# In the fourth step, VectorE takes the outputs of the third unit ahead of the last two pieces of words, and ScalarE scales the last piece behind the evictions of k and q

## The chip, the core and the metric

The kernel runs on one core of a Trainium2 chip. A core has five engines that run side by side and meet at semaphores: TensorE (PE in the profile, with PEld for its weight loads), VectorE (DVE), ScalarE (ACT), GpSimd (POOL) and SyncE (SP, which here only issues DMAs). Each engine works off its own queue in the order in which the program wrote it. The metric is the device time of one execution in microseconds (us); the time of a kernel is the median over its runs.

## The reference

Two blocks follow each other. The first is an mLSTM cell over 4 batches, 8 heads, 768 tokens and a head width of 40, written as a recurrence:

```python
m_new  = np.maximum(f[t] + m, i[t])
f_stab = np.exp(f[t] + m - m_new);  i_stab = np.exp(i[t] - m_new)
C = f_stab * C + i_stab * outer(v[t], k[t])
n = f_stab * n + i_stab * k[t]
y[t] = sigmoid(o[t]) * (C @ q[t]) / max(|n . q[t]|, 1)
```

Its output, seen as x with 3072 tokens of width 320, goes through a feed-forward block of width 1024, all in float32:

```python
h   = ((x @ w1) * (x @ w2)) @ w3
out = h @ w_out
```

The four weight matrices come as 64-bit floats. The kernel reads each number as two 32-bit words and makes a 32-bit float of them itself.

## The kernel before, in words

**Units and steps.** The 3072 tokens are cut into 24 units: unit n is a run of 128 tokens of one batch, all 8 heads. The main loop runs over 32 steps, s = 0 to 31. In step s TensorE, within `quarter_work`, computes the outputs of unit s-1 (products of its masked weights with v, and of q with the states: the tiles `ph` and `pi`, printed as `cell`), then the scores of unit s (`ss`) and its contributions to the state (`pc`). Behind them come the turning of y (`x_trans`, tile `px`) and of k and q of the next unit (`turn`, tile `pt`). Ahead of them come the matmuls of the feed-forward block that are due in the step: `up` multiplies x with 256 columns of w1 and of w2 over the first 256 of the 320 rows (tiles `pa` and `pb`), and `up_rest` adds the last 64 rows, for which the weights lie in a tile of their own, `wr` (line 623), and multiplies both results.

**The fourth and the fifth step.** "The fourth step" is s = 3; the third unit is n = 2, whose outputs are taken there. The feed-forward matmuls of s = 2 and 3 use columns 0 to 511 of the weights, those of s = 4 start on columns 512 to 1023 (f = 4, 5 of `ups`).

**The words.** A weight matrix is fetched in pieces of 512 columns (`fetch`). The ten pieces of w1, w2 and `wr` are listed in `w12`: columns 0 to 511 of w1 (two row blocks), of w2 (two) and of `wr`, and then the same for columns 512 to 1023. A piece is fetched as words into a `raw` tile by a DMA that SP issues, scaled by two instructions of ScalarE (`scale`, lines 188 and 192; `scale_next` takes the next fetched piece), and put together by two instructions of VectorE (`to_f32`, lines 196 and 197; `convert` takes the next scaled piece, and scales one itself if none is waiting). The last two pieces are the second row block of w2 (a tile printed as `w`) and `wr`, both for columns 512 to 1023. The `raw` tiles are four, used in turn; a fetch waits until VectorE is done with the piece that lay there.

**Who sets the order.** From `front` on, every engine but TensorE is held to the order in which the program wrote its instructions (`keep_order`, line 539), and TensorE has its own chain of order (`in_order`). So the place of a `convert()` in the text is its place in VectorE's queue. In step 3 both pieces are converted in `rest()` (lines 876 to 878), ahead of `outputs(2)`. VectorE's outputs are the instructions at lines 414, 421, 429, 431, 432, 434 and 436; between them stand the masking of the scores (line 390, needed by TensorE for the outputs of the next step), the state (lines 399 and 405, with GpSimd's decay at line 332 between them) and, at the end of the step, `rows_of_u` (line 292).

**Counters.** `n_cvt` says how many pieces are converted at the end of each step, and `converted` how many have been, which decides how far `fetch` runs ahead.

Of the kernel before, what the change touches and what calls it, by code (L numbers as in the profile page):

```python
# [16 lines left out]
def kernel(  # L17
# [166 lines left out]
    def scale(raw, early):  # L184


        lo, hi = raw[:, :, 0], raw[:, :, 1].bitcast(FP)
        nc.scalar.activation(out=hi, in_=hi, func=AF.Prelu, scale=2.0 ** -111, alpha=2.0 ** 32)
        if early:
            nc.vector.tensor_scalar(out=lo, in0=lo, scalar1=2.0 ** -29, scalar2=2.0 ** 23, op0=OP.mult, op1=OP.add)  # L190
        else:
            nc.scalar.activation(out=lo, in_=lo, func=AF.Copy, scale=2.0 ** -29, bias=2.0 ** 23)

    def to_f32(dst, raw):
        bits, V = dst.bitcast(U32), nc.vector
        V.tensor_scalar(out=bits, in0=raw[:, :, 1], scalar1=3, scalar2=None, op0=OP.logical_shift_left)
        V.tensor_tensor(out=bits, in0=bits, in1=raw[:, :, 0], op=OP.add)  # L197
# [32 lines left out]
    def scale_next(early=False):  # L230
        scaled.append(pend.pop(0))
        scale(scaled[-1][1], early)

    def convert():
        if not scaled:
            scale_next()
        dst, raw, ko, half = scaled.pop(0)
        if dst is not None:
            to_f32(dst, raw)
            return  # L240
        w3 = wst.tile([128, CW], FP, name="w3", tag="w3")
        to_f32(w3, raw)
        if half == 0:
            w3T_t[ko] = wst.tile([128, FO, 128], FP, name="w3T", tag="w3T")
        nc.vector.transpose(out=w3T_t[ko].rearrange("c k (m r) -> c m k r", r=32)[:, 2 * half:2 * half + 2],
                            in_=w3.rearrange("r (m c k) -> r m k c", m=2, k=FO))
        if half:
            turned_w3.append(ko)
# [59 lines left out]
    def turn(n):  # L308


        if n >= N_DVE:
            for src, dst, name in zip(turned_in[n % 2], (kT_t, qT_t), ("kT", "qT")):
                dst[n] = sb.tile([128, NP, P], FP, name=name, tag=name)
                done = nc.vector.transpose(out=dst[n].rearrange("i p (r f) -> i p f r", f=4),
                                           in_=src[:, 32:TB].rearrange("i (p f d) -> i p f d", p=NP, f=4)[:, :, :, 0:32])
            return done
        for src, dst, name in ((kbuf[n % NB], kT_t, "kT"), (qbuf[n % NBQ], qT_t, "qT")):
            pt = mps([128, NP, P], "pt")
            for p in range(NP):
                transpose(pt[:, p, :], src[:, 2 * p:2 * p + 2, :].rearrange("p a b -> p (a b)"))  # L320
            dst[n] = sb.tile([128, NP, P], FP, name=name, tag=name)
            nc.scalar.copy(out=dst[n], in_=pt)
# [9 lines left out]
        nc.gpsimd.tensor_tensor(out=new, in0=old, op=OP.mult, in1=decay[:, b * NP:(b + 1) * NP, 2 * c + x:2 * c + x + 1]  # L332
                                .to_broadcast([P, NP, D1]))

    def quarter_work(s, rest, between):


        rest()

        def part(j, c0, n):  # L340
            return cell[j][:, :, c0:c0 + NP * n].rearrange("p x (n d) -> p x n d", d=n)

        ss, pc, pi = part(0, 0, L), part(0, NP * L, D1), part(1, 0, D1)
        ph = [cell[1][:, x, NP * D1:2 * NP * D1].rearrange("p (h d) -> p h d", d=D1) for x in range(2)]
        n = s - 1
        if 0 <= n < NU:
            pw, vt, qT = u_t.pop(n), vbuf[n % NBV], qT_t.pop(n)
            before = before_t.pop(n)

            if n < N_DIAG:  # L350
                ph = mps([P, H, D1], "ph")
                for hq in range(H):
                    for r in halves:
                        mm(ph[r, hq, :], pw[r, hq, :], vt[r, hq, :])
            for hd in range(H // 2 if n >= N_DIAG else 0):
                for x, e in quarters:
                    hq = hd if x == e else hd + H // 2
                    mm(ph[x][halves[e], hd, :], pw[halves[x], hq, :], vt[halves[x], hq, :])
            for p in range(NP):
                for hip, x in quarters:  # L360
                    mm(pi[halves[x], hip, p, :], qT[heads[hip], p, halves[x]], before[x][heads[hip], p, :])
        den = None
        if 0 <= s - 1 < NU:
            den = outputs(s - 1, pi, ph)
            den()
            if between:
                for _ in range(3):
                    den()
                den = None
                between()  # L370
        n, first_read = s, None
        if n < NU:
            c, b = divmod(n, B)
            kt, vw = kbuf[n % NB], vw_t.pop(n)
            ends = range(2 if c < NT2 - 1 else 1)
            first, second, after = state[b]
            before_t[n] = first, second
            state[b] = after, second, first
            kT, qT, pw = kT_t.pop(n), qT_t[n], u_t[n]
            for p in range(NP):  # L380
                for hip, x in quarters:
                    mm(ss[halves[x], hip, p, :], kT[heads[hip], p, halves[x]], qT[heads[hip], p, halves[x]])
            M = D if n else L
            for p in range(NP):
                for x, e in quarters:
                    if x in ends:
                        mm(pc[e * L:e * L + M, x, p, :], kt[halves[x], 2 * p + e, 0:M], vw[halves[x], 2 * p + e, :])
        if n < NU:
            pv = pw.rearrange("p (n two) t -> p two n t", two=2)
            first_read = nc.vector.tensor_tensor(out=pv, in0=ss, in1=pv, op=OP.mult)  # L390
        with tc.issue_after(first_read.ins) if first_read else nullcontext():
            if den:
                den()
            if n < NU:

                if c:
                    nc.vector.tensor_tensor(out=second, in0=pc[:, 0], in1=second, op=OP.add)  # L397
                else:
                    nc.vector.tensor_copy(out=second, in_=pc[:, 0])
                if len(ends) > 1:  # L400
                    decayed(after, second, n, 1)
            if den:
                den()
            if n < NU and len(ends) > 1:
                nc.vector.tensor_tensor(out=after, in0=pc[:, 1], in1=after, op=OP.add)
            if den:
                done = den()
        return done if den else first_read
# [390 lines left out]
    n_out = [0] * 27 + [1, 0, 1, 0, 3]  # L799
    w12 = [("w12", i, part) for part in range(2) for i in range(2 * KF + 1)]  # L800
    todo = w12[5:] + [("wo", i, 0) for i in range(FO)] + [("w3", ko, part) for ko in range(FO) for part in range(2)]
    n_cvt = [0, 0, 2, 0, 1, 2, 3, 3, 3] + [2] * 6
    n_fetch = [5, 5, 10]
    pinned, ahead = 32, 9
    behind = ExitStack()
    turned, converted, fetched = 0, 2, 5

    for s in range(len(n_up)):
# [62 lines left out]
        def rest():  # L871
            for x in open_ups:
                up_rest(*x)
            if seven:
                seven[2]()
            if s == 3:
                for _ in range(2):
                    convert()

        def between():  # L880
            twice(1)
            weighted(2)
            rows_of_u(3)
            for _ in range(3):
                scale_next()
            for n in range(2):
                x_trans(n)
                if n == 0:
                    warm(5)
            for _ in range(3):  # L890
                convert()
            turn(2)
            block = up(*now[0])
            weighted(3)
            weights(3)
            masks(3)
            out_gate(2)
            convert()
            up_rest(*block)

        gated = None
        if s <= NU:
            gated = quarter_work(s, rest, between if s == 2 else None)
        else:
            rest()
        with tc.issue_after(gated.ins) if gated else nullcontext():
# [11 lines left out]
            if N_DVE <= s + 1 < NU:  # L918
                gated = turn(s + 1)
# [10 lines left out]
            cell_psum.close()  # L930
            banks.extend([ps_m] * 3 + [ctx.enter_context(tc.tile_pool(name="ps_x", bufs=4, space=bass.MemoryType.PSUM))] * 4)
        if s in (2, 3):
            turned, converted = 2, converted + (4 if s == 2 else 2)
        if s + 1 < N_DVE:
            while turned < min(s - 1, NY):
                x_trans(turned)
                turned += 1
            if s not in (1, 2):
                turn(s + 1)
        if s < NU:  # L940
            if 0 < s < NU - 1 and s != 2:
                if s != 1:
                    weighted(s + 1)
                weights(s + 1)
                if 2 < s < N_DVE:
                    twice(s - 1)
                masks(s + 1)
            if s != 2:
                out_gate(s)
# [50 lines left out]
```

## Time and profile before

| | |
|---|---|
| median of 3 runs | 429.05 us (428.34, 429.05, 430.54) |
| profiled execution, its own time | 428.51 us |
| its span on the engines | 426.5 us |
| mean granted TensorE clock | 0.988 |
| TensorE busy | 411.7 us (97%) |
| VectorE busy | 313.0 us (73%) |
| ScalarE busy | 149.7 us (35%) |
| GpSimd busy | 154.6 us (36%) |

The profile is of one execution. Its span runs from the first to the last instruction of the engines; 2.0 us of the execution's own time lie outside it. In a timeline each line has a start in us from the span's start, a duration in us, the engine, the line of the kernel, the operation and the tiles (written from read), how many instructions were merged into it, and in brackets how long the engine had stood idle before it and what ended that. A list of waits gives for each pair of waiter and releaser the total in us, the number of times and the longest. In a table by stretches each line has the busy time and number of instructions of each engine, then the granted TensorE clock as a share of full speed, then the busy share of the DMA engines and what they moved.

### The profile page before, as it was taken

How to read it: one execution, taken by the hardware profiler on the slowest of the kernel's cores; microseconds unless marked ns; L12 is line 12 of the kernel's file. 1: busy time of each engine (PE TensorE's matmuls, PEld its weight loads, DVE VectorE, ACT ScalarE, POOL GpSimd, SP SyncE). 2: the span in 40 equal slices, each digit the busy share in tenths (PEclk: the TensorE clock that was granted, in tenths of full speed). 3: DMA queues.
4: the chain of work that ended last, by engine and by line, in shares of the span. 5: the costliest groups of instructions: out<-in, count | busy, mean ns of one | idle time of the engine just before them, and what ended most of it. 6: DMA issues, size and time to landing. Idle time of an engine off the chain costs nothing.

```text
span 426.5 us, 13080 instructions
## 1 busy us (share of the span) xinstructions
PE 411.7 (97%) x5353; PEld 337.9 (79%) x5353; DVE 313.0 (73%) x634; ACT 149.7 (35%) x404; POOL 154.6 (36%) x211
## 2 busy tenths in 40 slices
PE   7799789999999999999999999999999999999996
PEld 5788678887688788787777778788778779888896
DVE  6676787888949769778736966596878699575971
ACT  4866665567724523630333313132311110210000
POOL 4530232233303203303307743646363587542100
PEclk9879999999999999999999999999999999999999
DMA  8989878597997775886435585656421120000001
GB/s 189 227 169 233 210 126 147 132 197 180 210 205 135 166 181 132 179 162 111 83 85 129 136 147 129 142 135 113 96 39 36 35 38 2 31 2 31 2 32 61
DMA packets 135211, 51.15 MB, mean 120 GB/s; under 512 B 109360, under 2 KB 126960, under 8 KB 135152
## 3 DMA queue, kind: packets, MB, share of 16 engines
q1 hardware_dynamic: 131552, 46.29, 52.7%
q10 hardware_dynamic: 3600, 4.03, 2.7%
q8 instruction: 42, 0.69, 0.7%
q14 instruction: 17, 0.14, 0.1%
HBM read 44.50 MB, written 5.80 MB: 118 GB/s over the span
## 4 chain that ended last, share of the span: by engine, by line
PE 77%; DVE 7%; issue 5%; DMA 5%; SPq 4%; ACT 1%; POOL 0%; DVEq 0%; POOLq 0%; ACTq 0%
PE cell L92 20%; PE pa L92 18%; PE pb L92 12%; PE wp L92 8%; PE o L92 8%; PE po L92 4%; PE p L92 3%; DVE w3T L654 1%; DMA wo<-in_moe_w_dram 1%; PE px L95 1%; SPq L150 1%; DMA yb<-y_d 1%; DMA y_d<-y 1%; PE pt L95 1%; DMA out_dram<-o_sb 1%
## 5 line engine op out<-in xcount | busy, mean ns | idle before, releaser
L332 POOL TENSOR_TENSOR state<-state,decay 128x164 f32<-128x164 f32 x40 | 20.0, 499 | 156.6 <-DVE state L397 101.3
L92 PE MATMUL pa<-xT,w 128*128 128x256 f32 x240 | 60.4, 382 | 0.0
L92 PEld LDWEIGHTS pa<-xT,w 128*128 128x128 f32 x240 | 44.4, 190 | 6.4
L300 ACT ACTIVATE pw<-pw,aT 128x64 f32<-128x64 f32 x184 | 46.4, 337 | 3.2 <-ACT o_sb L729 1.4
L92 PE MATMUL pb<-xT,w 128*128 128x256 f32 x192 | 45.4, 379 | 0.0
L717 POOL TENSOR_TENSOR ab<-ab,a_sb 128x512 f32<-128x512 f32 x22 | 29.4, 1358 | 32.0 <-DVE ab L672 32.0
L92 PEld LDWEIGHTS pb<-xT,w 128*128 128x128 f32 x192 | 36.5, 190 | 5.0
L699 POOL TENSOR_TENSOR wo<-wo 128x512 f32<-128x512 f32 x22 | 27.5, 1270 | 31.4 <-DVE wo L674 31.4
L92 PE MATMUL pa<-xT,wr 64*64 64x256 f32 x384 | 37.0, 386 | 0.5 <-DVE wr L197 0.5
L92 PE MATMUL wp<-wo,w3T 128*128 128x320 f32 x128 | 35.9, 433 | 1.2 <-issue 0.7
L305 POOL TENSOR_SCALAR_AFFINE_SELECT pw<-pw 64x512 f32<-64x512 f32 x48 | 35.8, 745 | 2.2 <-ACT pw L300 0.6
L92 PE MATMUL pb<-xT,wr 64*64 64x256 f32 x384 | 36.4, 380 | 0.0
L92 PE MATMUL cell<-w3o,ab 128*128 128x320 f32 x128 | 35.4, 432 | 0.0
L626 ACT ACTIVATE a_sb<-pa 128x512 f32<-128x512 f32 x24 | 14.3, 596 | 58.9 <-PE pb L92 58.9
L92 PEld LDWEIGHTS wp<-wo,w3T 128*128 128x128 f32 x128 | 23.8, 190 | 10.7 <-issue 1.0
L627 DVE TENSOR_TENSOR ab<-pb,a_sb 128x512 f32<-128x512 f32 x24 | 16.4, 687 | 21.5 <-ACT a_sb L626 21.3
L92 PEld LDWEIGHTS cell<-w3o,ab 128*128 128x128 f32 x128 | 24.3, 190 | 9.5
L92 PEld LDWEIGHTS pa<-xT,wr 64*64 64x64 f32 x384 | 18.9, 132 | 15.5 <-issue 8.8
L421 DVE TENSOR_TENSOR h<-cell,h 64x164 f32<-64x164 f32 x88 | 28.7, 326 | 1.6
L674 DVE SCALAR_TENSOR_TENSOR a_sb<-pa,wo 128x512 f32<-128x512 f32 x12 | 8.3, 689 | 28.1 <-PE pa L92 28.1
L92 PE MATMUL po<-w3o,ab 128*128 128x320 f32 x96 | 26.4, 433 | 0.0
L92 PEld LDWEIGHTS po<-w3o,ab 128*128 128x128 f32 x96 | 18.1, 190 | 7.3
(179 smaller groups left out, 844.4 us busy)
## 6 DMA issues: line engine op xcount, KB each, us to landing
raw<-in_moe_w_dram SPq DMA_DIRECT2D x64, 128.0 KB, 3.2
kbuf<-in_k_dram SPq DMA_DIRECT2D x24, 160.0 KB, 4.1
v_all<-in_v_dram SPq DMA_DIRECT2D x24, 160.0 KB, 4.5
o_in<-in_o_gate_dram SPq DMA_DIRECT2D x24, 160.0 KB, 5.0
pw<-U_d SPq DMA_DIRECT2D x28, 128.0 KB, 3.4
raw<-in_moe_w_dram SPq DMA_DIRECT2D x5, 512.0 KB, 5.6
raw<-in_moe_w_out_dram SPq DMA_DIRECT2D x8, 320.0 KB, 4.2
gates<-in_k_dram SPq DMA_DIRECT2D x28, 80.0 KB, 3.0
```

The lines of the kernel that those rows point to most:

```text
L92: in_order(nc.tensor.matmul(out, lhsT=lhsT, rhs=rhs, start=start, stop=stop))
L95: in_order(nc.tensor.transpose(out, in_, ident[0:n, 0:n]))
L150: nc.sync.dma_start(out=o_t[n], in_=rows(o_gate, n))
L300: nc.scalar.activation(out=pw[:, h, :], in_=src[:, h, :], func=AF.Exp, bias=aT[:, c, b * H + h:b * H + h + 1])
L305: nc.gpsimd.affine_select(out=pw[r], in_=pw[r], compare_op=OP.is_ge, fill=0.0, base=0, pattern=[[0, H], [1, L]], channel_multiplier=-1)
L332: nc.gpsimd.tensor_tensor(out=new, in0=old, op=OP.mult, in1=decay[:, b * NP:(b + 1) * NP, 2 * c + x:2 * c + x + 1] .to_broadcast([P, NP, D1]))
L421: nc.vector.tensor_tensor(out=part, in0=ph[x][halves[e]], in1=part, op=OP.add)
L626: nc.scalar.mul(out=a_sb, in_=pa, mul=UP ** -2)
L627: nc.vector.tensor_tensor(out=ab_t[gr][j][:, fs[0]:fs[-1] + 1, t0:t0 + a_sb.shape[-1]], in0=pb, in1=a_sb, op=OP.mult)
L674: nc.vector.scalar_tensor_tensor(out=out, in0=p, scalar=UP ** -2, in1=q, op0=OP.mult, op1=OP.add)
L699: aside_by.tensor_tensor(out=kept[j][:, 1:4:2], in0=kept[j][:, 1:3], in1=kept[j][:, 3:4].to_broadcast([128, 2, TH]), op=OP.add)
L717: aside_by.tensor_tensor(out=t[:, f:FO:FH, :], in0=t[:, f:FO:FH, :], in1=a, op=OP.mult)
```

## The change

In step 3 VectorE's queue is rearranged. Before, it ran: both pieces of words, outputs of unit 2 (first part), masking of the scores of unit 3, the rest of the outputs interleaved with the state, `rows_of_u`. Now it runs: first part of the outputs (lines 414, 421, 429), the w2 piece, masking of the scores, the rest of the outputs with the state, `rows_of_u`, and then the `wr` piece, which became the conversion at the end of the step. On ScalarE the w2 piece is scaled where both were; the `wr` piece is scaled after the two evictions of `turn(4)` (kT and qT). The order of the instructions on TensorE, GpSimd and SP is unchanged; four semaphore waits of TensorE on VectorE in the fifth step, behind the one on `wr`, are no longer written, since what they waited for now stands ahead of `wr` in VectorE's queue.

```diff
-    def quarter_work(s, rest, between):
+    def quarter_work(s, rest, between, late):
...
                 den = None
                 between()
+            if late:
+                late()
         n, first_read = s, None
...
-    n_cvt = [0, 0, 2, 0, 1, 2, 3, 3, 3] + [2] * 6
+    n_cvt = [0, 0, 2, 1, 1, 2, 3, 3, 3] + [2] * 6
...
             if s == 3:
-                for _ in range(2):
-                    convert()
+                scale_next()
...
-            gated = quarter_work(s, rest, between if s == 2 else None)
+            gated = quarter_work(s, rest, between if s == 2 else None, convert if s == 3 else None)
...
-            turned, converted = 2, converted + (4 if s == 2 else 2)
+            turned, converted = 2, converted + (4 if s == 2 else 1)
...
             if s not in (1, 2):
                 turn(s + 1)
+            if s == 3:
+                scale_next()
```

## The prediction

> **What bounds the kernel now.** I read the page's busy times first, then TensorE's waits, then VectorE's and TensorE's timelines around the fourth and fifth steps, and last the granted clock there.
>
> The page:
>
> ```profile
> PE 411.7 (97%) x5353; PEld 337.9 (79%) x5353; DVE 313.0 (73%) x634; ACT 149.7 (35%) x404; POOL 154.6 (36%) x211
> ```
>
> TensorE is busy for 97% of the span. Past 60 us it has hardly an idle moment: the longest waits there are of 0.7, 0.5 and 0.4 us. So what TensorE loses before 60 us it has no slack to win back.
>
> TensorE's waits over the whole span, total, times, longest:
>
> ```profile
> PE cell L92 <- issue: 3.1, 3, 1.5
> ...
> PE pa L92 <- DVE wr L197: 0.5, 1, 0.5
> ...
> PE px L95 <- DVE y L436: 0.2, 1, 0.2
> ```
>
> The 0.5 us on `wr` and the 1.5 us are in the fifth step. VectorE's timeline there:
>
> ```profile
> 40.40 0.68 DVE L627 TENSOR_TENSOR ab<-pb,a_sb 128x512 f32<-128x512 f32 x1
> 41.00 0.42 DVE L196 TENSOR_SCALAR w<-raw 128x512 uint32<-128x512 uint32 x1
> 41.56 0.69 DVE L197 CUSTOM_DVE_ANT_0 w<-raw,w 128x1024 uint16<-128x1024 uint16 x1
> 44.29 0.43 DVE L196 TENSOR_SCALAR wr<-raw 128x512 uint32<-128x512 uint32 x1 [2.04 <-ACT raw L188]
> 44.86 0.69 DVE L197 CUSTOM_DVE_ANT_0 wr<-raw,wr 128x1024 uint16<-128x1024 uint16 x1
> 45.47 0.49 DVE L414 TENSOR_TENSOR h<-cell,gT 128x328 f32<-128x328 f32 x1
> ...
> 47.46 0.68 DVE L390 TENSOR_TENSOR pw<-cell,pw 128x512 f32<-128x512 f32 x1
> ```
>
> VectorE stands idle for 2.04 us for the words of `wr`, with the third unit's outputs queued behind, although their products were done at about 39.8. That idle time is what the change fills. But TensorE:
>
> ```profile
> 43.18 1.89 PE L92 MATMUL pb<-xT,w 128*128 128x256 f32 x8
> 45.61 0.43 PE L92 MATMUL pa<-xT,wr 64*64 64x256 f32 x1 [0.54 <-DVE wr L197]
> ...
> 48.24 0.68 PE L92 MATMUL cell<-v_all,pw 64*64 64x41 f32 x32 [1.54 <-issue]
> ...
> 50.71 0.54 PE L95 MATMUL px<-ident,y 128*128 128x128 f32 x3 [0.20 <-DVE y L436]
> ```
>
> In its order TensorE needs `wr` first (45.61, 0.06 us after its conversion ends at 45.55), then the masked scores of line 390 (end 48.14; TensorE goes on at 48.24, so I put the 1.54 us "issue" down to it), then y. The new order makes line 390 early and `wr` late, and `wr` comes first.
>
> [...] the table by 2 us stretches shows
>
> ```profile
> 14.00:16.00 2.00, 0.67 (x15) 0.43 (x15) 1.79 (x4) 2.00 (x9) 0.00 (x0) 1.00 1.05 298
> 16.00:18.00 2.00, 2.00 (x93) 2.00 (x93) 1.45 (x3) 1.59 (x6) 1.93 (x4) 0.78 1.12 287
> 18.00:20.00 2.00, 1.14 (x50) 0.99 (x44) 1.77 (x6) 1.50 (x7) 0.49 (x1) 0.50 1.23 192
> ...
> 46.00:48.00 2.00, 0.70 (x16) 0.18 (x8) 1.92 (x6) 2.00 (x10) 0.00 (x0) 1.00 1.04 166
> ```
>
> a clock (third number from the end) of 0.50 after a thin stretch that was not even wholly idle, full again only in 26:28; and 1.00 at 46:48, where the gaps were 0.54 and 1.54 us. [...] line 197 on 128x1024 took 0.69 us alone and 1.00 at 29.66, beside a product of GpSimd. [...]
>
> **The change part by part.**
>
> VectorE until `wr`. All starts are taken from the durations and spacings above. From 41.00, the first part of the outputs: line 414 to the end of line 429's slot was 45.47 to 47.46 = 1.99, so line 196 on w starts at 42.99. The w2 piece: 44.29 to 45.47 before for the same two operations, 1.18, so line 390 starts at 44.17 instead of 47.46. From line 390 to the end of `rows_of_u` was 47.46 to 51.11, where the next instruction began: 3.65, with GpSimd's decay in it (0.47 wait). So `wr`'s line 196 starts at 47.82. Its words landed at 43.58 and ScalarE is done at 44.82 as before ( the evictions of kT and qT, 0.47 apart, now pass it while it waits for the landing), so the move on ScalarE costs nothing and the cover is 3.0 us.
>
> `wr` itself: 1.26 us alone (44.29 to 45.55), end 49.08. But GpSimd runs `masks(4)` from 0.7 us after y begins (50.07 to 50.81 before), hence at about 47.51 to 48.89, then a decay to 49.4. Beside such work line 196 on 128x320 took 0.61 instead of 0.32, and line 197 on 128x640 0.74 instead of 0.49: +0.29 and +0.25. Low bound 0, high bound +0.6 (0.74 and 1.00 for the large forms, the longest seen); I take +0.54, end 49.62.
>
> TensorE. Before `wr`: `pb` needs the w2 piece from its second product on, at 43.4; it is ready at 44.24, so 0.8 us of stall inside `pb`, which ends near 45.7. That is ahead of the wait on `wr` and costs nothing more. Then idle until 49.68. `up_rest` to the first outputs is 0.92 (55.50 to 56.42 one step later), the four cell parts 1.82 (69.74 to 71.56), without the waits on line 390 and y. So px starts at 49.68 + 0.92 + 1.82 = 52.42 instead of 50.71: **+1.71 us**, +1.17 without the sharing on GpSimd. Removed: 0.54 + 1.54 + 0.34 (48.70 to 49.50 against 0.46 in an undisturbed step) + 0.20 of waits; added: one wait of about 4.0.
>
> What is queued behind. On TensorE the whole fifth step, for which ScalarE (a_sb) and VectorE (lines 627, 414) wait in turn; VectorE gets to line 627 at about 51.3 instead of 51.11, and its next masked scores at about 53.9, before TensorE needs them at 58.1. On SP the fetch of the fourth w_out piece waits for `wr`'s tile: issued at 48.5 before, 49.7 now, +1.2 us for k, q and v of unit 6 behind it. Those were issued at 49.0 to 49.5, land some 5.7 later, and are turned at 60.3 (61.9 now): hidden, with 5 us of cover. GpSimd, the kT and qT evictions and y are earlier, which nobody uses while TensorE waits.
>
> The clock. [...] Bounds: [...] 5.1 if it stays low for 10.2 us as at 17 to 27 us. I take +1.6[...].
>
> Sum against the profiled execution's own 428.51: + 1.71 + 1.6 = 431.8. This execution lies 0.54 under the median of its three; the highest, 430.54, is 2.0 above it, which a clock drop in the thinner gap of before would explain, so I add nothing for it.
>
> **The rivals.**
>
> *The stall without the clock drop* (0.28): 428.51 + 1.2 to 1.7 = 429.7 to 430.2. For it: the gap of before left the clock alone. Against: the gap is now more than twice as long.
>
> *The stall is soaked up* (0.09). At 58.2 TensorE stands 1.22 us for "issue" in the middle of one kind of product[...]: 1.71 - 1.22 = +0.5, 429.0. [...]
>
> *Not slower, by late words* (0.09). `wr`'s words set the start of before (landing 43.58, then 2.0 us to TensorE), while the new order has 3.0 us of cover. In an execution where they land later, before loses one for one and the new order nothing: at 1.7 us later both are equal, at 3.8 later the new order is 2.1 faster, 426.9. Against: the landing took 5.7 us, and other loads of this stage lie between 3.5 and 8.0. Nor can the change "free" TensorE by line 390 alone: `wr` stands ahead of it.
>
> *A long clock drop* (0.06): up to 428.51 + 1.7 + 5.1 = 435.3.
>
> **How the numbers follow.** My forecast[...] has 0.48: 431.8, its own range 430.9 to 433.7. The range for all takes in the plain stall and half of the soaked-up case: 429.3 to 434.0. A change of 0.5% is 2.1 us, about what a measurement tells from none, so slower begins at 431.2. That holds for nearly all of the forecast and the long drop, and a little of the plain stall when other runs sit 0.5 higher: 0.56. Same: 0.40, the rest of the plain stall, the soaked-up case and half of the late words. Faster: 0.04, the latest words.
>
> **What would show it.** In the profile of the changed kernel: line 390 of unit 3 at about 44.2; `wr`'s line 197 ending at 49.1 to 49.7; one wait of TensorE on `wr` of 3.4 to 4.0 us in place of 0.54 and 1.54; px at about 52.4; a granted clock of 0.5 in the 50 to 54 us region. The prediction is wrong if TensorE's wait on `wr` is under 2 us, if the gap at 58.2 shrinks by what was lost, or if the clock stays at 1.00 in most runs, which leaves only the stall.

## The result and the profile after

| | before | after |
|---|---|---|
| median of 8 runs | 429.19 us (427.95 to 430.61) | 432.01 us (431.17 to 433.29) |
| profiled execution, its own time | 428.51 us | 431.84 us |
| its span on the engines | 426.5 us | 429.8 us |
| mean granted TensorE clock of that execution | 0.988 | 0.987 |

The ratio is 1.0064, with a 95% interval of 1.0038 to 1.009: slower by 2.8 us or 0.64%. The interval reaches a little below the 0.5% from which the prediction speaks of slower; two further measurements below (E7, the same kernel again, 1.0071, and E2, 1.0067) agree with it. Lines 371 to 876 of before stand two further down in the changed kernel, so 390 is now 392, 414 is 416 and 436 is 438. The page, busy times:

```profile
PE 411.8 (96%) x5353; PEld 337.6 (79%) x5353; DVE 314.7 (73%) x634; ACT 149.6 (35%) x404; POOL 155.5 (36%) x211
```

TensorE did the same 5353 products in the same busy time, 0.1 us more. The span grew by 3.3 us, so TensorE waited for about 3.2 us more. (Both executions spend 10 to 11 us at half clock in all, so this sum doesn't show the clock's part; the table by stretches below does.) Its list of waits (total, times, longest):

```profile
PE pa L92 <- DVE wr L197: 4.3, 2, 3.8
...
PE cell L92 <- issue: 1.8, 2, 0.9
...
PE pb L92 <- DVE w L197: 0.9, 1, 0.9
```

The wait on `wr` has grown from 0.5 to 3.8, and 0.9 on the w2 piece is new; of the "issue" waits the 1.5 has gone. VectorE's timeline:

```profile
40.85 0.49 DVE L416 TENSOR_TENSOR h<-cell,gT 128x328 f32<-128x328 f32 x1
...
43.53 0.43 DVE L196 TENSOR_SCALAR w<-raw 128x512 uint32<-128x512 uint32 x1 [0.61 <-ACT raw L188]
...
44.70 0.69 DVE L392 TENSOR_TENSOR pw<-cell,pw 128x512 f32<-128x512 f32 x1
...
48.35 0.78 DVE L196 TENSOR_SCALAR wr<-raw 128x512 uint32<-128x512 uint32 x1
49.26 0.91 DVE L197 CUSTOM_DVE_ANT_0 wr<-raw,wr 128x1024 uint16<-128x1024 uint16 x1
```

The outputs now fill VectorE's idle 2 us and the scores are masked 2.8 us earlier, but `wr` is ready 4.6 us later (50.17 against 45.55). TensorE's timeline:

```profile
44.84 1.56 PE L92 MATMUL pb<-xT,w 128*128 128x256 f32 x6 [0.85 <-DVE w L197]
50.23 0.64 PE L92 MATMUL pa<-xT,wr 64*64 64x256 f32 x1 [3.82 <-DVE wr L197]
...
54.57 0.55 PE L95 MATMUL px<-ident,y 128*128 128x128 f32 x3
...
63.02 0.35 PE L92 MATMUL cell<-vw,kbuf 64*40 64x41 f32 x12 [0.94 <-issue]
```

`px` moved from 50.71 to 54.57, by 3.86. From `wr`'s first product to `px` took 4.34 us, where the forecast had put 0.92 + 1.82 = 2.74. The table by stretches of 2 us, busy times by engine (TensorE first) and the granted clock third from the end, shows why:

```profile
48.00:50.00 2.00, 0.00 (x0) 0.00 (x0) 1.86 (x3) 0.47 (x2) 1.77 (x4) 1.00 1.21 238
50.00:52.00 2.00, 1.77 (x20) 1.12 (x24) 0.17 (x1) 0.00 (x0) 0.49 (x1) 0.58 1.00 364
52.00:54.00 2.00, 2.00 (x92) 2.00 (x87) 0.80 (x2) 0.60 (x1) 0.00 (x0) 0.57 1.20 266
54.00:56.00 2.00, 2.00 (x68) 1.95 (x60) 1.89 (x7) 0.83 (x2) 0.00 (x0) 1.00 1.50 145
```

and one line of the same table of before:

```profile
52.00:54.00 2.00, 2.00 (x12) 1.77 (x11) 1.89 (x7) 2.00 (x8) 0.65 (x2) 1.00 1.15 237
```

TensorE stands still through 48:50 and then works at half clock from about 50.3 to 53.7 (0.58 and 0.57 are 1.7 us each), 3.4 us in all, as in no stretch of before past 28 us, where the clock is 1.00 up to 420. Up to `px` the wait thus costs twice: its own length, and 1.6 us of slower work behind it. Half clock stands behind the wait on `wr` in all three profiles with this order: 3.4 us in this one and in E2, 6.8 in E7.

### The profile page after: what moved, and what is told of

Its sections match the earlier page's. It is cut to its first block, busy times and chain, and to the rows that moved or that the text cites. A ratio compares the mean times of both kernels' runs of the same rounds, so it can differ in the third digit from the quotient of the medians.

```text
span 429.8 us, 13078 instructions
## 1 busy us (share of the span) xinstructions
PE 411.8 (96%) x5353; PEld 337.6 (79%) x5353; DVE 314.7 (73%) x634; ACT 149.6 (35%) x404; POOL 155.5 (36%) x211
## 4 chain that ended last, share of the span: by engine, by line
PE 71%; issue 11%; DVE 7%; DMA 4%; POOL 4%; SPq 2%; ACT 1%; DVEq 0%; POOLq 0%; ACTq 0%
PE cell L92 20%; PE pa L92 19%; PE pb L92 12%; PE o L92 8%; PE wp L92 6%; PE p L92 3%; DVE w3T L656 2%; POOL pw L305 1%; POOL raw L649 1%; DMA wo<-in_moe_w_dram 1%; PE px L95 1%; PE pt L95 1%; DMA y_d<-y 1%; POOL state L332 1%; PE ph L92 1%
## 5 line engine op out<-in xcount | busy, mean ns | idle before, releaser
L628 ACT ACTIVATE a_sb<-pa 128x512 f32<-128x512 f32 x24 | 14.3, 597 | 62.5 <-PE pb L92 62.5
L92 PE MATMUL po<-w3o,ab 128*128 128x320 f32 x96 | 26.4, 433 | 0.0
```

Source lines behind the costliest of these rows:

```text
L92: in_order(nc.tensor.matmul(out, lhsT=lhsT, rhs=rhs, start=start, stop=stop))
L628: nc.scalar.mul(out=a_sb, in_=pa, mul=UP ** -2)
```

## The experiments

Diffs are against the changed kernel, E4's against the kernel before. E1 to E4 ran beside each other on one chip, E5 to E7 on one, E8 to E11 on one. The last column is each kernel's mean time at half clock over all its timed executions, from the span and mean granted clock of each: (1 - clock) x 2 x span. Before has 10.1, 10.4 and 9.4 us in these three sessions.

| | kernel | median, us | before beside it | ratio, 95% interval | at half clock, us |
|---|---|---|---|---|---|
| E1 | both pieces behind the outputs' first part | 427.17 | 429.11 | 0.9964 [0.9943, 0.9984] | 8.7 |
| E2 | changed, ScalarE's order as before | 431.4 | 429.11 | 1.0067 [1.0046, 1.0089] | 14.3 |
| E3 | changed, 14 small products in the gap | 431.07 | 429.11 | 1.004 [1.002, 1.006] | 8.6 |
| E4 | before, 6 such products | 432.04 | 429.11 | 1.0061 [1.0037, 1.0084] | 7.6 |
| E5 | changed, 4 wide products in the gap | 432.9 | 429.36 | 1.0084 [1.0058, 1.0109] | 9.3 |
| E6 | `wr` behind the masking | 426.6 | 429.36 | 0.9934 [0.9917, 0.995] | 5.9 |
| E7 | changed, again | 432.68 | 429.36 | 1.0071 [1.0046, 1.0097] | 17.2 |
| E8 | changed, TensorE takes `wr`'s products later | 429.54 | 429.17 | 1.0004 [0.9979, 1.003] | 10.5 |
| E9 | E6 with the same move | 428.34 | 429.17 | 0.9969 [0.995, 0.9988] | 8.7 |
| E10 | E6 again | 427.1 | 429.17 | 0.9962 [0.9946, 0.9978] | 7.9 |
| E11 | E1 again | 428.31 | 429.17 | 0.9982 [0.9963, 1.0001] | 9.0 |

The theory: `wr`, which TensorE needs first, was put behind work it needs later, so TensorE stalls and its clock drops. The rivals: the stall alone does it; the stall is soaked up further on and something else costs; ScalarE's part of the change costs.

### E1 and E11: `wr` not last

```diff
             if s == 3:
-                scale_next()
+                for _ in range(2):
+                    scale_next()
+
+        def late():
+            for _ in range(2):
+                convert()
...
-            gated = quarter_work(s, rest, between if s == 2 else None, convert if s == 3 else None)
+            gated = quarter_work(s, rest, between if s == 2 else None, late if s == 3 else None)
...
-            if s == 3:
-                scale_next()
```

with the two counters set for it. The outputs' first part keeps its new place; only `wr` comes forward.

> The changed kernel, but the wr piece is converted directly behind the w2 piece, ahead of the masking of the scores (ScalarE scales both where before did). The third unit's outputs still come first. Theory (the loss is wr's late place alone, with the clock drop that its gap brings): wr is converted by about 45.5 to 46 us as in before, the masked scores about 46.2 to 46.7 instead of 48.1, so TensorE's second wait of the fifth step (1.5 us) goes too: 1.2 to 1.9 us faster than before, 427.3 to 428.0. Rival (taking the outputs ahead of the words costs in itself, by the stall of the w2 piece or by ScalarE): no faster than before, 429 to 431.

> The kernel with wr converted directly behind the w2 piece, ahead of the masking, once more beside the others. Theory (the earlier wr, the better): 0.3 us or more faster than with wr behind the masking. Rival (the masking, which TensorE needs right after wr, is as urgent, and early masking also covers late words): as fast or slower.

Measured: 427.17 and 428.31, ratios 0.9964 and 0.9982. TensorE's timeline of E1:

```profile
46.58 0.43 PE L92 MATMUL pa<-xT,wr 64*64 64x256 f32 x1
...
49.69 0.54 PE L95 MATMUL px<-ident,y 128*128 128x128 f32 x3 [0.21 <-DVE y L438]
```

No wait on `wr` long enough to be listed, and `px` 1.0 us ahead of before, though this execution began the step 1.6 later (43.03 against 41.45). Against the changed kernel E1 is some 4 us faster (ratios 0.9964 against 1.0067 for E2 beside it). So the place of `wr` is the whole loss; taking the outputs ahead of the words is itself a gain of 0.9 to 1.9 us by the two medians (E11's interval just reaches no gain).

### E2: ScalarE's order as before

```diff
             if s == 3:
-                scale_next()
+                for _ in range(2):
+                    scale_next()
...
-            if s == 3:
-                scale_next()
```

> The changed kernel, with ScalarE's order of before: both pieces are scaled ahead of the evictions of kT and qT; VectorE's order stays the changed one. Theory (the move on ScalarE costs nothing, the scaled words wait for VectorE anyway): within 0.3% of the changed kernel, 431.0 to 433.0. Rival (the later scaling is part of the loss): 1 us or more faster than the changed kernel, below 430.8.

Measured: 1.0067, against 1.0064 and 1.0071 for the changed kernel. ScalarE's half of the change costs nothing and brings nothing that can be measured. In E2's trace the evictions of kT and qT stand behind the scaling of `wr` again (46.32), but VectorE took `wr` only at 50.55, in 0.64 + 0.91 us. TensorE's wait and the half clock behind it are there too (0.78, 0.50 and 0.87 in the three stretches of 52 to 58, 3.4 us in all):

```profile
52.29 0.43 PE L92 MATMUL pa<-xT,wr 64*64 64x256 f32 x1 [3.65 <-DVE wr L197]
```

```profile
54.00:56.00 2.00, 2.00 (x88) 2.00 (x84) 1.40 (x3) 0.23 (x1) 0.00 (x0) 0.50 1.22 261
```

Its times can't be set beside before's one by one: this execution reached the fifth step's first products at 45.03, before's at 41.45.

### E3, E4, E5: filling TensorE's gap

These ask for the clock's share by giving TensorE products that nobody reads. They add work and leave none out.

```diff
 E3   def rest():
+        if s == 4:
+            for _ in range(14):
+                mm(cell[1][:, 0, 328:328 + P], ident, ident)
...
 E4 (kernel before)   def rest(): ... up_rest(*x)
+        if s == 4:
+            for _ in range(6):
+                mm(cell[1][:, 0, 328:328 + P], ident, ident)
...
 E5   def rest():
+        if s == 4:
+            for _ in range(4):
+                mm(cell[0][:, 0, 0:448], ident, w1[:, 0, 0:448])
```

> The changed kernel, with 14 products of 128x128 (identity by identity, into columns that nobody reads) on TensorE ahead of its wait on wr, about 3.0 us of work in a gap of about 3.9. They compute nothing that is used. Theory (about half of the loss is the halved clock after the gap): no stretch of 0.50 behind 50 us, and 1.2 to 2.0 us faster than the changed kernel, 430.0 to 430.8. Rival (the loss is the wait alone, the clock drop costs nothing that is not hidden): as the changed kernel, 431.5 to 432.5, or slower by the added work.

> The kernel before, with 6 such products on TensorE between wr's products and the outputs of the fifth step, about 1.3 us of work in a gap of 1.54. Theory (the spread of before, 428.0 to 430.6, is a clock drop in the gap of the fifth step in about half of its executions): all executions lie within about 1 us of 428.4, median 428.0 to 428.6. Rival (the spread is from elsewhere, such as the first 30 us): spread and median as before, 429.0 to 429.4.

> The changed kernel with TensorE's gap ahead of wr filled by only 4 products of 448 columns (identity by w1, into columns of the scores that the next scores overwrite), about 3.0 us of work in 8 instructions and their weight loads, where the earlier filling took 56[...]. They compute nothing that is used. Theory (the clock drop after the gap costs about as much as the wait): fewer microseconds at half clock than the changed kernel by 3 to 5, no half clock at 50 to 54 us in most executions, and 0.8 to 1.7 us faster than the changed kernel run beside it. Rival (the drops behind the gap are hidden, the loss is the wait alone): less time at half clock and within 0.5 us of the changed kernel.

None of the three decided it by its time. E3 measured 431.07, only 0.3 under E2 beside it, and E5 432.9, 0.2 above the changed kernel (E7) beside it: both spent less time at half clock, and neither won the time that the theory gave; E5's lies where the rival had put it. The traces show why that doesn't settle it. TensorE's timeline of E3:

```profile
45.74 3.29 PE L92 MATMUL cell<-ident 128*128 128x128 f32 x28
49.59 0.43 PE L92 MATMUL pa<-xT,wr 64*64 64x256 f32 x1 [0.57 <-DVE wr L197]
...
55.01 0.80 PE L95 MATMUL pt<-ident,kbuf 128*128 128x128 f32 x3 [2.02 <-issue]
```

The gap is filled, and the clock stayed at 1.00 through 50:54. Then TensorE stood 2.02 us for no engine, in the middle of one kind of product, and the clock fell behind that instead: 0.69 in 54:56, 0.50 in 56:58. E4 was badly aimed. Its fill writes into the bank that the third unit's outputs still occupied, and waited for VectorE to read them:

```profile
46.52 1.60 PE L92 MATMUL cell<-ident 128*128 128x128 f32 x12 [0.69 <-DVE h L421]
48.06 0.68 PE L92 MATMUL cell<-v_all,pw 64*64 64x41 f32 x32
...
57.38 0.25 PE L92 MATMUL cell<-vw,kbuf 64*40 64x41 f32 x7
58.43 0.46 PE L92 MATMUL cell<-vw,kbuf 64*40 64x41 f32 x25 [0.79 <-issue]
...
96.12 0.23 PE L92 MATMUL cell<-vw,kbuf 64*40 64x41 f32 x1 [1.68 <-issue]
```

The fill itself cost nothing by `px` (49.93 against 50.71 in before); the time went later, in waits like the 1.68 us at 96.12. Its executions spread further than before's (428.73 to 436.5), against what was expected. Whether before's own thin gap at 46.5 to 48.2 ever costs it the clock stays open; in its one profile it didn't (1.00 in 46:50). E5 used a quarter of the instructions. TensorE's timeline of E5:

```profile
46.44 3.27 PE L92 MATMUL cell<-w,ident 128*128 128x448 f32 x8 [0.21 <-DVE state L407]
...
52.61 0.55 PE L95 MATMUL px<-ident,y 128*128 128x128 f32 x3
...
98.75 0.66 PE L95 MATMUL pt<-ident,kbuf 128*128 128x128 f32 x4 [1.49 <-DVE den L431]
```

Here the clock was 1.00 from 48 to 54, and `px` came at 52.61, 1.90 behind before instead of 3.86. Against the changed kernel's profile `px` is 1.96 us earlier; 0.36 of that is `wr`'s products starting at 49.87 instead of 50.23, and 1.6 is the clock. But E5 lost it again further on, most of it in the 1.49 us at 98.75, and its time is no better. E3 and E5 show the clock's share where it arises and fail to show it in the total: what it is worth in the end is not shown by them.

### E7: the changed kernel again

> The changed kernel once more, beside the two others on the same chip. Theory: 431.2 to 432.3, with 12 to 15 us at half clock in the mean, 3 to 5 more than the kernel before. Rival (its extra half clock is an accident of one profile): as much half clock as before, about 10 us.

Measured: 432.68, ratio 1.0071, again slower, a little above what was expected, and with 17.2 us at half clock. TensorE's timeline of E7:

```profile
49.49 0.43 PE L92 MATMUL pa<-xT,wr 64*64 64x256 f32 x1 [3.69 <-DVE wr L197]
...
53.66 0.90 PE L95 MATMUL px<-ident,y 128*128 128x128 f32 x3
...
61.11 0.62 PE L92 MATMUL cell<-v_all,pw 64*64 64x41 f32 x32
...
62.93 0.55 PE L95 MATMUL px<-ident,y 128*128 128x128 f32 x3
```

TensorE's timeline of before, for the fifth and sixth steps:

```profile
41.45 1.89 PE L92 MATMUL pa<-xT,w 128*128 128x256 f32 x8
...
56.42 0.62 PE L92 MATMUL cell<-v_all,pw 64*64 64x41 f32 x32
...
57.82 0.39 PE L92 MATMUL cell<-vw,kbuf 64*40 64x41 f32 x19
59.42 0.35 PE L92 MATMUL cell<-vw,kbuf 64*40 64x41 f32 x13 [1.22 <-issue]
59.71 0.55 PE L95 MATMUL px<-ident,y 128*128 128x128 f32 x3
```

and E7's table by stretches:

```profile
52.00:54.00 2.00, 2.00 (x78) 1.92 (x74) 1.62 (x6) 0.00 (x0) 0.00 (x0) 0.50 1.21 315
54.00:56.00 2.00, 2.00 (x11) 2.00 (x10) 1.50 (x7) 0.97 (x2) 0.60 (x2) 0.50 1.39 128
```

The clock is down from about 50.4 to 57.2 (0.61 in 50:52, 0.69 in 56:58), 6.8 us, twice the 3.4 of the changed kernel's profile. The outputs at 61.11 are 4.69 behind before's 56.42, and 1.5 of that came back: the 1.22 us for which before stands for "issue" at 59.42 is missing here, and `px` of that step is only 3.22 late (62.93 against 59.71). More comes back further on: at the end the span is 428.3 against 426.5, 1.8 longer.

### E8: the stall without the clock drop

```diff
     def quarter_work(s, rest, between, late):
-        rest()
+        if s != 4:
+            rest()
...
             if late:
                 late()
+            if s == 4:
+                rest()
         n, first_read = s, None
```

In the fifth step TensorE takes the outputs of unit 3, whose masked scores are early now, ahead of `wr`'s products. The number of instructions is the same.

> The changed kernel, with TensorE's products on wr in the fifth step moved behind the outputs of that step (both engines' instructions are the same in number; VectorE's line 629 moves behind its first outputs with them). VectorE's and ScalarE's order around wr stays the changed one. Theory (the loss is TensorE standing still until wr, and the half clock after it): the outputs, 0.9 us of work, go into the gap, which falls from 3.9 to about 3.0 us; 0.9 us faster than the changed kernel by that and up to 1.6 more where the clock then stays up: 429.5 to 431.3. Rival (the place of wr on TensorE does not matter, the loss is VectorE's new order): within 0.5 us of the changed kernel, 431.5 to 432.7.

Measured: 429.54 against 429.17, ratio 1.0004. TensorE's timeline of E8:

```profile
42.08 1.89 PE L92 MATMUL pa<-xT,w 128*128 128x256 f32 x8
...
50.64 0.43 PE L92 MATMUL pa<-xT,wr 64*64 64x256 f32 x1 [2.61 <-DVE wr L197]
52.44 0.55 PE L95 MATMUL px<-ident,y 128*128 128x128 f32 x3
...
59.98 0.55 PE L95 MATMUL px<-ident,y 128*128 128x128 f32 x3
```

and its stretch behind the wait:

```profile
52.00:54.00 2.00, 2.00 (x61) 1.93 (x51) 1.95 (x7) 1.40 (x3) 0.00 (x0) 1.00 1.01 247
```

The wait, now broken by 1.2 us of work, is followed by no drop of the clock in this profile (1.00 from 48 to 58), and over all executions E8's 10.5 us at half clock are near before's 9.4. `px` is 1.73 us behind before. That this is nearly the 1.71 of the prediction is luck: E8's execution was already 0.63 behind when the step began (42.08 against 41.45), so the step itself added 1.1. But it shows what a delay of that size is worth: at the next `px` it has shrunk from 1.73 to 0.27 (before's 1.22 us of "issue" at 59.42 does not occur), and in the median 0.4 us is left, with an interval of -0.9 to +1.3. So the stall alone costs little in the end, which points to the clock drop for most of the changed kernel's 2.3 to 3.3 us. The share is argued, not shown: E8 also shortens the stall (in the changed kernel's profile it is 2.26 at `px` without the clock's 1.6), and E3 and E5, which kept the clock up behind the wait, did not win the time back.

### E6, E10 and E9: a better order

E6 is E1 with `wr` converted one place further back, directly behind the masking of the scores.

```diff
-                scale_next()
+                for _ in range(2):
+                    scale_next()
...
         with tc.issue_after(first_read.ins) if first_read else nullcontext():
+            if late:
+                late()
             if den:
                 den()
...
-            if s == 3:
-                scale_next()
```

E9 is E6 with E8's move.

> The changed kernel with the wr piece converted directly behind the masking of the scores (line 392), ahead of the rest of the outputs: the place between the early one of the first experiment and the changed kernel's. Theory (TensorE's fifth step starts when wr is ready, so its time moves with wr's place one for one): wr is ready at about 46.2 to 46.7, TensorE's wait is about 0.5 to 1.0 us, nothing follows it, and the time lies 0.3 to 0.9 us above the first experiment's, 427.5 to 428.1. Rival (any order with wr behind the masking is slower than before): above 429.1.

> The kernel with wr converted directly behind the masking of the scores, once more, beside the two others and the early one. Theory: 2.0 to 2.9 us faster than before, as measured, 426.2 to 427.2. Rival (the first reading was six lucky executions): 1.2 to 1.9 faster, as first expected.

> The kernel with wr converted behind the masking of the scores, and TensorE's products on wr in the fifth step moved behind that step's outputs. A try at a better version: the remaining wait of TensorE on wr, 0.67 us, is covered by the outputs, but the next scores then wait for the state's last sum on VectorE. Theory: 0.2 to 0.6 us faster than the version without the move. Rival (TensorE there already waits for nothing that an order can hide): the same within 0.3 us.

E6 measured 426.6 and, as E10, 427.1; E11 beside E10 took 428.31. I had expected E6 0.3 to 0.9 us behind E1, since one operation more stands ahead of `wr`; it was ahead both times, by 1.2 us where the two ran side by side, though the intervals of those two ratios overlap. TensorE's timeline of E6:

```profile
46.50 0.43 PE L92 MATMUL pa<-xT,wr 64*64 64x256 f32 x1 [0.67 <-DVE wr L197]
...
49.23 0.55 PE L95 MATMUL px<-ident,y 128*128 128x128 f32 x3
```

and VectorE's:

```profile
45.18 0.43 DVE L196 TENSOR_SCALAR wr<-raw 128x512 uint32<-128x512 uint32 x1 [0.36 <-ACT raw L188]
```

VectorE still waits 0.36 us for the words of `wr`, so the masking ahead of it was done in time that would have been idle, and y no longer holds up `px`. Less time at half clock (5.9 and 7.9 us against 8.7 and 9.0) goes the same way; but neither is shown to be the cause: in the profiles of the repeat, E11 has `px` at 48.72, ahead of E10's 49.51. E9 missed. I had expected it ahead of E6; it took 1.2 us more than E10. VectorE's reading of the `wr` products (line 634) now stands behind its first outputs, at 51.02 instead of 49.69 in E10, and the next matmuls into those banks wait 1.62 us for it. TensorE's timeline of E9:

```profile
51.76 2.00 PE L92 MATMUL pa<-xT,w 128*128 128x256 f32 x8 [1.62 <-DVE ab L634]
```

That this wait is the 1.2 us is not shown: at the next `px` E9's profile (58.15) lies 0.47 behind that of E6 (57.68), the order of E10, which stood 0.66 us for "issue" just ahead of it.

E6 is the best order found: 0.9934 and 0.9962 of before.

## Why the prediction was right, and where it wasn't

**The direction and the cause** were right. TensorE sets the time, `wr` is what it needs first, and making line 390 early frees nothing while `wr` stands ahead of it. E1 against E2 shows that the place of `wr` alone makes the difference. No profile with the changed order (this one, E7, E2, E8) has VectorE waiting for `wr`'s words, so the rival of late words did not come up in them.

**VectorE until `wr`.** Line 390 was forecast at 44.17 and came at 44.70; `wr`'s line 196 at 47.82, came at 48.35. Both are late by one thing that the sum lacked: VectorE waited 0.61 us for the w2 words. The working kept the timing of these words from before. ScalarE took them up at 40.09 there and at 42.83 in the changed kernel. In E7 VectorE took them at 42.93 without a wait, and `wr`'s products start at 49.49, 0.19 ahead of the forecast, so this term belongs to one execution and not to the kernel.

**Sharing with GpSimd.** Forecast +0.54 on 1.26 us, measured +0.56 (48.35 to 50.17 is 1.82), and +0.43 in E2 and E8. GpSimd's timeline after:

```profile
48.19 1.44 POOL L305 TENSOR_SCALAR_AFFINE_SELECT pw<-pw 64x512 f32<-64x512 f32 x2
```

It runs beside the conversion, as forecast, and a decay (49.72 to 50.49) beside the rest. The traces show a slowing: line 196 took 0.78 us here and 0.64 in E2 and E8 instead of 0.43, line 197 0.91 instead of 0.69.

**TensorE's wait.** Forecast about 4.0 after 0.8 on the w2 piece; 3.82 after 0.85. The 2.74 us from `wr`'s first product to `px` at full clock came out as 2.74 in E5 and 2.73 in E6. The list of waits removed and added in that paragraph (2.62 against 4.8) does not give +1.71 but 2.2; the forecast was made from the starts, not from this list.

**What is queued behind, and ScalarE** at no cost: E2 agrees.

**The clock.** Forecast one short drop, +1.6. That figure was my estimate: the profile of before shows one stretch of half clock, of 10.2 us, and no wait of TensorE above 1.6. In the profile `px` lies 4.34 behind `wr`'s first product instead of 2.74, so 1.6, with 3.4 us at half clock. In E7 it was 6.8 us, about 3.2 by the same measure, part of the way to the rival of a long drop. Over all executions the changed kernel spends 6.8 us (E7) and 4.2 us (E2) more at half clock than before beside it; the first measurement has 13.2 us, 3.1 more than before has beside E1 to E4 (before's clocks of that first measurement are not on record). That is 3.4, 2.1 and 1.6 us of TensorE work if all of it counts. So the term was right for the profiled execution and rather small for the median. That all of it counts isn't shown: among 151 executions of before, 3.4 us more at half clock go with only 0.5 to 0.7 us. Where the profile of before shows half clock, it lies in the opening (17.1 to 27.3 us), and there it seems to cost less than behind the wait on `wr`: the changed kernel's profile has only 6.8 us of it there (19.6 to 26.4) and yet began the fifth step no earlier (41.66 against 41.45).

**The stall.** This is the term that failed. "+1.71" was carried to the end unreduced, and the rival that it is soaked up had 0.09. E8 shows a stall of that size given back almost wholly by 59.98, and E7 and E2 gave back 1.5 there; the changed kernel's profile only 0.28 (the wait put down to "issue" shrank from 1.22 to 0.94). What the rival supposed, that the delay goes into before's 1.22 us of "issue", thus came about in three of four profiles; what TensorE waits for there is not shown. "No slack past 60 us" was wrong as well: E7's 3.22 us had shrunk to 1.8 by the end. That the sum came out at 431.8 beside 432.01 owes something to two errors of opposite sign: a stall that lasts less than was put down, and a clock drop that is longer in many executions.

**"I add nothing"** for the spread of before was off by 0.7 us. Before, too, spends about 6.8, 10.2 or 13.7 us at half clock in most of its executions (113 of 151), with medians of 428.5, 429.2 and 429.8. But its median of 429.19 lies 0.7 above the execution that the sum started from, which had 10.2 us itself. The forecast, made from that execution, is low by as much, and this hid part of the stall's shortfall.

## What to carry to other kernels

When a queue is rearranged to fill an idle stretch, look first at the order in which the engine that sets the time consumes what the queue produces; here the filled 2 us cost a 3.8 us wait, because the piece needed first was put last, and with that piece directly behind the masking of the scores the same idea wins 0.4 to 0.7%. Price a wait of TensorE by whether the clock survives it: E8 still waited 2.6 us for `wr`, but with 1.2 us of work in the middle of the gap; its clock stayed at 1.00, and it lost nothing measurable. A delay of 1 to 2 us is not a loss until it is followed past the next place where the engine waits for something else.

## What was unexpected of the hardware

Time at half clock came in portions of about 3.41 us: the profiles show stretches of 3.4 us (the changed kernel, E2, E3), 6.8 (the changed kernel's opening, E7) and 10.2 (before's opening), apart from a piece at the very end, and in three quarters of the 343 timed executions (259) its sum is a whole number of portions to within a tenth. Their number varies from run to run of the same kernel: from none (6 executions) to five or more (16) in the 151 of before.

Products added in an idle gap were followed by a new wait. The 28 matmuls that the profile shows for E3's fill took 3.3 us in the gap, and yet TensorE then stood 2.02 us for "issue" at 55.01; in before it stands 1.22 at 59.42. In four profiles these waits keep their place in TensorE's queue: before waits behind the 19th product `cell<-vw,kbuf`, E4 with 12 matmuls more ahead of it behind the 7th; the changed kernel behind the 20th, E5 with 8 more behind the 12th:

```profile
59.73 0.32 PE L92 MATMUL cell<-vw,kbuf 64*40 64x41 f32 x12
60.78 0.43 PE L92 MATMUL cell<-vw,kbuf 64*40 64x41 f32 x20 [0.74 <-issue]
```

On the DMA queue that the profile lists as instruction, one packet of 0.02 MB ended at 57.98 in before and one at 61.50 in the changed kernel, 1.4 and 1.5 us before TensorE went on; that TensorE waited for it is not shown. In E2, E7 and E8 TensorE doesn't stand there at all.
